# Every batch fetches its expert's weights, in place of looking for the expert in the slots of the last three batches

## The chip, the cores and the metric

The kernel runs on one core of one Trainium2 chip. The metric is the device time of one execution in microseconds (us), the median of several runs. The core's engines are called as in the profile: PE (matmuls) with PEld (its weight loads), DVE, ACT, POOL and SP; POOL, ACT and SP also issue DMAs, all of which run on the core's 16 DMA engines.

## What is computed

Eight batches of 576 tokens go through causal attention with forget gates (8 heads of 64), and each batch's result (576 x 512) through one expert of eight. The expert is chosen once for a whole batch, from the mean of its attention output:

```python
x = attention(q, k, v, f)                  # (8, 576, 512)
pooled = x.mean(axis=1)
logits = pooled @ w_gate                   # (8, 8)
e_idx = argmax(logits, axis=1)             # one expert for a batch
gate_w = softmax(logits)[e_idx]
h = relu(x[b] @ w1[e_idx[b]])              # 512 -> 1024
out[b] = gate_w[b] * (h @ w2[e_idx[b]])    # 1024 -> 512
```

With the inputs of all runs here the eight batches choose the experts 2, 4, 3, 3, 3, 5, 5, 3. An expert has 512 x 1024 weights in w1 and as many in w2, in fp32 in HBM: 4.2 MB, which become 2.1 MB of bf16 in SBUF.

## The kernel before

A batch `b` has two quads `g = 2b, 2b+1` of four heads. The stages of a quad: its K and Q are loaded by POOL's DMA queue (`rawk`, `rawq`, L290, fp32 to bf16 pieces), transposed on DVE (`kt`, `qt`, L406), scores are made on PE in four steps S (`ps_s`, L419), exponentiated on ACT (`e`, L425), masked on POOL (L434; two quads share the masks with DVE, L432), and multiplied by V on PE (P, L459). V (`vf`, loaded from the SP and ACT queues, L302) is first weighed by the forget gates on POOL (`vb`, L443, L446). DVE normalizes into `xT` (L479). After a batch's second quad come the gate (`gate1` to `gate7`: L566, L571, L575, L581, L590), the expert's number in POOL's registers and its weights (`weights1`, L605), then the hidden layer H on PE (L645, with relu on DVE and ACT, L653 and L655), and the output O (L662, L665), which is copied (L672, L674) and stored by SP (L679).

The order on every engine is made when the program is built: `Order.run` (L144) gives each operation a cost, a priority and, for loads, a landing time on shared DMA engines (L107), and takes the best that is ready; the result is a fixed instruction order. Rings of buffers bound how far work runs ahead: four pairs of raw tiles, two of `qt`/`kt`, two of `vf`, three weight slots `w`. Of POOL's order around the weights: `raws[g]` is issued behind the first weighing of V of quad g-2 (L706), and a batch's weights as soon as `gate3` has the expert (L696, priority -5). [...]

Weights live in three slots used in turn. Batch 0 loads w1 in eight pieces (L615) and w2 (L638). Batch 1 has one older batch and simply fetches: `fetch` (L596) issues three DMAs from HBM, two for w1 (L601), one for w2 (L602). From batch 2 on POOL compares the expert with those of up to three batches before, puts the answers together as bits of a number, and switches (L626) over 2, 4 or 8 arms:

```python
        for n in range(1, min(3, b - 1) + 1) if CACHE else ():
            bit = (ev[b] == ev[b - n]) * (1 << (n - 1))
            case = bit if case is None else case + bit
        if case is None:
            fetch(b)
            return
        for arm in tc.Switch({mybir.EngineType.Pool: case}, 1 << min(3, b - 1)):
            if arm == 0:
                fetch(b)
            elif arm < 4:
                z = wslot[b - (1 if arm % 2 else 2)]
                for q in range(2):
                    nc.gpsimd.dma_start(W1[w][:, 2 * q:2 * q + 2, :], W1[z][:, 2 * q:2 * q + 2, :], max_dma_last_dim=2048)
                nc.gpsimd.dma_start(W2[w], W2[z], max_dma_last_dim=2048)
```

Arm 0 fetches; a match one or two batches back copies the slot in SBUF (L632, L633); a match only three batches back needs nothing, since that is the same slot. With the experts above, batch 2 takes arm 0, batches 3, 4 and 6 copy, batch 5 takes arm 0, and batch 7 finds its slot filled. The other engines have a branch for each switch too (L905).

Of the kernel before, what the change touches and what calls it, by code (L numbers as in the profile page):

```python
# [34 lines left out]
MAX_SPAN = 72.0  # L35
COLD = 1.35
HIT = .07
CACHE = 1
VGRAIN = .022

MASKS = (2, 3)
# [190 lines left out]
def fast_path(ctx, tc, q, k, v, f, moe_w_gate, moe_w1, moe_w2, out, flag):  # L232
# [359 lines left out]
    def gate7(op, b):  # L592
        i, ps = od.slot(("gate", b)), PS_W[od.slot(("bank", ("spread", b)))]
        nc.vector.tensor_copy(GATE[i], ps[:, 0:1])
# [10 lines left out]
    def weights1(op, b, a):  # L605
        i, w = od.slot(("gate", b)), od.slot(("w", b))
        if a == 0:
            wslot[b] = w
            assert b < 3 or wslot[b - 3] == w
            ev[b] = nc.gpsimd.value_load(IDX8[i][0:1, 0:1], min_val=0, max_val=NE - 1)  # L610
        if b == 0:
            src = moe_w1[bass.ds(ev[b], 1), :, :].rearrange("o (q p t) n -> p (o q) t n", p=P, t=2)
            parts = W1[w].rearrange("p a (m n) -> p a m n", m=4)
            for q in range(2):
                nc.gpsimd.dma_start(parts[:, a, 2 * q:2 * q + 2, :], src[:, q, :, 256 * a:256 * a + 256])  # L615
            return


        case = None
# [15 lines that stand above are left out]
    def weights2(op, b):  # L635
        w = od.slot(("w", b))
        if b == 0:
            nc.gpsimd.dma_start(W2[w].rearrange("p (a m) n -> p a (m n)", a=4),  # L638
                                moe_w2[bass.ds(ev[b], 1), :, :].rearrange("o (a p m) n -> p (o a) (m n)", a=4, m=2))
# [46 lines left out]
    for b in range(NB):  # L686
# [8 lines left out]
        g7 = od.add(f"g7{b}", "DVE", .1, lambda op, b=b: gate7(op, b), prio=-5, after=[g6], gives=(("bank", ("spread", b)),))  # L695
        ld = lx = od.add(f"W{b}", "POOL", 2.9 if b and CACHE else 1.7, lambda op, b=b: weights1(op, b, 0), prio=-5, after=[g3], takes=(("w", b),), lands=5.4 * (1 - CACHE * HIT * min(3, max(0, b - 1))) if b else 1.5, grain=.17 if b else .05)  # L696
        if b == 0:
            quarters = [ld]
            for a in (1, 2, 3):
                lx = od.add(f"W{b}{a}", "POOL", 1.3, lambda op, b=b, a=a: weights1(op, b, a), prio=-5, behind=[lx], lands=1.5, grain=.05)  # L700
                quarters.append(lx)
        ld2 = od.add(f"w{b}", "POOL", .01 if b else .6, lambda op, b=b: weights2(op, b), prio=-5, behind=[lx], lands=5.3 * (1 - CACHE * HIT * min(3, max(0, b - 1))), grain=.17)
        if b == 0:
# [206 lines left out]
```

## Time and profile before

| what | value |
|---|---|
| median of 3 runs | 280.4 us (278.5 to 281.73) |
| the profiled execution, its own time | 278.5 us |
| its span, first to last instruction | 276.8 us |
| mean granted PE clock | 0.943 |
| busy: PE, ACT, DVE, POOL | 234.4, 167.8, 134.3, 114.9 us |
| HBM read, written | 45.25, 9.44 MB |
| weight fetches from HBM / copies in SBUF / neither | 4 (batches 0, 1, 2, 5) / 3 (3, 4, 6) / 1 (7) |

The span is read as stages by when POOL loads the expert's number (L610): 29.9 us for batch 0, then 53.6, 89.8, 116.8, 145.6, 175.2, 205.1 and 235.5 us for batch 7. After the last one only the FFNs of the last batches remain. In rows of the page "busy" is time in instructions, without waits, branches and DMA issue by the queues; a row's "idle before" names what the engine waited for, and "issue" there means that the profile shows nothing that it waited for.

### The profile page before, as it was taken

The numbers are of one execution on the slowest core, as the hardware profiler recorded it, in microseconds if no ns is written. First come the engines' busy times: TensorE is split into PE (matmuls) and PEld (weight loads), VectorE is DVE, ScalarE is ACT, GpSimd is POOL, SyncE is SP. The second block draws the span as 40 slices with busy tenths as digits, with TensorE's granted clock in tenths as the row PEclk, the third lists the DMA queues.
The fourth block names the chain that finished last, engine by engine and source line by source line (L and its number), as shares of the span: only waits on it lengthen the run. The fifth ranks groups of instructions, "written<-read, shape, count | busy, mean of one in ns | idle before, by whom it ended". The sixth has DMA issues, their size and how long they took to land.

```text
span 276.8 us, 8026 instructions
## 1 busy us (share of the span) xinstructions
PE 234.4 (85%) x3275; PEld 149.4 (54%) x3294; DVE 134.3 (49%) x350; ACT 167.8 (61%) x291; POOL 114.9 (42%) x181
## 2 busy tenths in 40 slices
PE   0889779799989758995999699986999499999991
PEld 0346347545965334771568445773457275794940
DVE  4977875733568613551187315762475153340500
ACT  2677878577638827863758656773577444452530
POOL 4375490051995353136933582439503921000000
PEclk9999999999999965998999979997999779999999
DMA  6994699999999999449893994799726301303132
GB/s 126 225 217 75 103 148 207 228 208 247 264 159 206 192 211 220 75 128 300 170 240 110 289 165 134 161 191 207 177 79 228 118 2 59 116 6 120 51 100 82
DMA packets 56208, 43.92 MB, mean 159 GB/s; under 512 B 39696, under 2 KB 42768, under 8 KB 56144
## 3 DMA queue, kind: packets, MB, share of 16 engines
q0 software_dynamic: 12240, 24.12, 44.3%
q1 hardware_dynamic: 31424, 15.90, 22.2%
q10 hardware_dynamic: 12480, 3.15, 5.7%
q8 instruction: 28, 0.46, 0.7%
q14 instruction: 36, 0.29, 0.4%
HBM read 45.25 MB, written 9.44 MB: 198 GB/s over the span
## 4 chain that ended last, share of the span: by engine, by line
PE 60%; issue 13%; POOL 9%; ACT 7%; DMA 6%; DVE 2%; POOLq 1%; ACTq 0%; DVEq 0%
PE ps_w L662 19%; PE ps_w L645 15%; PE ps_w L459 11%; PE ps_s L419 10%; ACT e L425 6%; POOL e L434 4%; DMA rawk<-in_k_dram 4%; PE ps_w L665 3%; POOL vb L443 2%; DMA w1e<-in_moe_w_dram 2%; POOL w1e L632 1%; DVE xT L479 1%; PE ps_w L571 1%; POOL w2e L633 1%; ACT lr L469 1%
## 5 line engine op out<-in xcount | busy, mean ns | idle before, releaser
L425 ACT ACTIVATE e<-ps_s 128x896 bf16<-128x896 f32 (+2 forms) x128 | 100.0, 833 | 28.0 <-PE ps_s L419 27.4
L645 PE MATMUL ps_w<-xT,w1e 128*128 128x288 bf16 x512 | 73.0, 295 | 1.0 <-DMA w1e<-in_moe_w_dram 1.0
L434 POOL TENSOR_SCALAR_AFFINE_SELECT e<-e 128x512 bf16<-128x512 bf16 (+1 forms) x72 | 42.0, 595 | 63.5 <-ACT e L425 51.9
L645 PEld LDWEIGHTS <-w1e 128*128 128x128 bf16 x512 | 60.5, 140 | 10.8 <-issue 5.4
L662 PE MATMUL ps_w<-w2e,h1T 128*128 128x512 bf16 x238 | 59.4, 385 | 1.8 <-issue 1.3
L419 PE MATMUL ps_s<-qt,kt 32*128 32x448 bf16 (+4 forms) x768 | 47.8, 308 | 12.6 <-DVE mid L368 7.7
L653 DVE TENSOR_SCALAR h1T<-ps_w,gate_b 128x288 bf16<-128x288 f32 x77 | 39.1, 516 | 36.4 <-PE ps_w L645 35.7
L479 DVE SCALAR_TENSOR_TENSOR xT<-ps_w,lr 128x256 bf16<-128x256 f32 (+1 forms) x64 | 27.0, 454 | 48.8 <-PE ps_w L459 26.1
L459 PE MATMUL ps_w<-e,vb 128*32 128x320 bf16 (+4 forms) x1024 | 34.5, 278 | 6.2 <-POOL vb L443 4.2
L662 PEld LDWEIGHTS <-h1T 128*128 128x128 bf16 x256 | 22.7, 98 | 29.2 <-issue 5.7
L419 PEld LDWEIGHTS <-kt 32*128 32x128 bf16 x768 | 20.2, 98 | 33.0 <-issue 21.8
L655 ACT ACTIVATE h1T<-ps_w,gate_b 128x288 bf16<-128x288 f32 x51 | 25.2, 500 | 20.2 <-PE ps_w L645 14.2
L674 ACT COPY otile<-ps_w 128x512 f32<-128x512 f32 (+1 forms) x29 | 16.0, 550 | 30.9 <-PE ps_w L662 27.7
L459 PE MATMUL ps_w<-e,WB 128*32 128x192 bf16 (+4 forms) x512 | 20.4, 269 | 13.3 <-POOL e L434 13.2
L459 PEld LDWEIGHTS <-vb 128*32 128x32 bf16 x1024 | 23.8, 106 | 13.4 <-POOL vb L443 4.7
L443 POOL TENSOR_TENSOR vb<-vf,WF 128x512 bf16<-128x512 f32 x25 | 26.1, 1046 | 2.8 <-ACT WF L380 2.5
L406 DVE STREAM_TRANSPOSE kt<-rawk 128x576 f32<-128x576 f32 (+1 forms) x17 | 21.2, 1248 | 10.1 <-PE ps_s L419 5.3
L464 ACT ACTIVATE lr<-ps_w 128x256 f32<-128x256 f32 (+1 forms) x31 | 12.7, 410 | 20.1 <-PE ps_w L459 19.8
L459 PEld LDWEIGHTS <-WB 128*32 128x32 bf16 x512 | 11.4, 100 | 24.1 <-issue 21.9
L406 DVE STREAM_TRANSPOSE qt<-rawq 128x576 f32<-128x576 f32 (+1 forms) x17 | 21.2, 1248 | 0.1
L672 DVE COPY otile<-ps_w 128x512 f32<-128x512 f32 (+1 forms) x11 | 6.8, 619 | 17.6 <-PE ps_w L662 15.2
L469 ACT ACTIVATE lr<-lr 128x256 f32<-128x256 f32 (+1 forms) x31 | 13.7, 443 | 1.0
(63 smaller groups left out, 117.0 us busy)
## 6 DMA issues: line engine op xcount, KB each, us to landing
out_dram<-otile SPq DMA_DIRECT2D x32, 256.0 KB, 2.3
rawk<-in_k_dram POOLq DMA_DIRECT2D x15, 288.0 KB, 4.7
rawq<-in_q_dram POOLq DMA_DIRECT2D x15, 288.0 KB, 6.6
w2e<-in_moe_w_dram POOLq DMA_DIRECT2D x4, 1024.0 KB, 15.0
vf<-in_v_dram SPq DMA_DIRECT2D x12, 256.0 KB, 9.1
vf<-in_v_dram ACTq DMA_DIRECT2D x12, 256.0 KB, 7.1
w1e<-in_moe_w_dram POOLq DMA_DIRECT2D x6, 512.0 KB, 8.7
w1e<-w1e POOLq DMA_DIRECT2D x6, 512.0 KB, 4.0
```

The lines of the kernel that those rows point to most:

```text
L406: nc.vector.transpose(dst, raw)
L419: nc.tensor.matmul(ps[:, col:col + i1 - i0], kt[32 * h:32 * h + 32, KLO[c]:KLO[c] + P, r], qt[32 * h:32 * h + 32, i0:i1, r], start=(r == 0 ...
L425: nc.scalar.activation(e[:, 2 * n:2 * n + 2, :], PS_S[od.slot(("s", (g, s, n)))][:, :, 0:WIDTH[s]], AF.Exp, scale=0.125)
L434: nc.gpsimd.affine_select(out=x, in_=x, pattern=[[0, 4], [1, n]], channel_multiplier=-1, base=base, compare_op=ALU.is_ge, fill=0.0)
L443: eng.tensor_tensor(vb[:, c, :, :], vf[:, c, h, :], WF[:, b, c, h].unsqueeze(3).to_broadcast([P, 2, 4, D]), op=ALU.mult)
L459: nc.tensor.matmul(ps[32 * h:32 * h + 32, lo - i0:hi - i0], lhs, e[s][:, h, col:col + hi - lo], start=(n == 0), stop=(n == len(parts) - 1) ...
L469: nc.scalar.activation(LR[i][:, 0:w], LR[i][:, 0:w], AF.Exp, scale=-1.0)
L479: nc.vector.scalar_tensor_tensor(XT[od.slot(("x", b))][:, mm, i0:i1], ps[:, 0:i1 - i0], 1.0 if (g, blk) in ON_DVE else LN_SCALE, LR[od.slo ...
L645: nc.tensor.matmul(ps[:, 0:288], lhs, xT[:, m, 288 * half:288 * half + 288], start=(m == 0), stop=(m == 3))
L653: nc.vector.tensor_scalar(dst, ps[:, 0:288], g[:, 0:1], 0.0, op0=ALU.mult, op1=ALU.max)
L655: nc.scalar.activation(dst, ps[:, 0:288], AF.Relu, scale=g[:, 0:1])
L662: nc.tensor.matmul(ps, h[:, j, P * sb:P * sb + P], r, start=(j == 0), stop=(j == 7))
```

## The change

One constant is changed.

```diff
-CACHE = 1
+CACHE = 0
```

It is used in three places. In `weights1` (L620) no comparison is made, `case` stays `None`, and every batch from 1 on calls `fetch`: the switch, its arms and the branches on the other engines are not in the program any more, and neither are the copies. In the planner (L696, L702) the issue of a batch's weights on POOL is costed at 1.7 instead of 2.9, and their landing is no longer shortened for likely matches. The planner therefore makes another order from batch 2 on. The start, up to the fetch of batch 1 and quads 4 and 5, is the same. On POOL, K and Q of quad 9 stood ahead of batch 2's weights and now stand behind them; K and Q of quad 10 stay behind batch 3's weights; at batch 4's weights, Q of quad 12 stood behind and both tiles of quad 12 and K of quad 13 now stand ahead, with Q of 13 behind; at batch 5's weights, both tiles of quad 14 stood behind and now only Q does. On PE the same matmuls are made, in a somewhat different mixing of S, P, H and O; behind the last gate stood 4 O and 16 H of batches 5 and 6 with all of batch 7, and now stand 14 H of batch 6, its O, and all of batch 7.

## Prediction

> **What bounds the kernel now.** First the page: its first line and three rows of its slices (6.9 us each).
>
> ```profile
> span 276.8 us, 8026 instructions
> ...
> PE   0889779799989758995999699986999499999991
> ...
> POOL 4375490051995353136933582439503921000000
> PEclk9999999999999965998999979997999779999999
> DMA  6994699999999999449893994799726301303132
> ```
>
> PE is nearly full from the second slice on, but for dips near slices 13-14, 18, 22, 26-27 and 31. Each is followed by a dip of PE's clock, and POOL is full right after each. DMA is full up to slice 15 and then is not. So PE is the bound, with holes, and the holes have to do with POOL. The waits of PE between 90 and 235.5 us say it outright:
>
> ```profile
> PE ps_w L459 <- POOL e L434: 12.9, 9, 3.6
> PE ps_w L459 <- POOL vb L443: 4.2, 3, 2.7
> ```
>
> 17.1 us in total, and next comes ACT with 1.6 us: P waits for masks and weighed V from POOL. POOL is 42% busy, so it isn't slow but late. Its timeline around batch 1's fetch, which has no switch, and around batch 5's, which is the same three DMAs in arm 0 of a switch:
>
> ```profile
> 54.81 1.44 POOL L601 DMA_DIRECT2D w1e<-in_moe_w_dram  x2 [12.98 <-DVE sumexp L585]
> 56.25 0.76 POOL L602 DMA_DIRECT2D w2e<-in_moe_w_dram  x1
> 57.01 0.65 POOL L434 TENSOR_SCALAR_AFFINE_SELECT e<-e 128x512 bf16<-128x512 bf16 x1
> ```
>
> ```profile
> 177.65 1.49 POOL L601 DMA_DIRECT2D w1e<-in_moe_w_dram  x2 [2.05 <-DVE h1T L653]
> 179.13 0.76 POOL L602 DMA_DIRECT2D w2e<-in_moe_w_dram  x1
> 184.75 0.63 POOL L434 TENSOR_SCALAR_AFFINE_SELECT e<-e 128x512 bf16<-128x512 bf16 x1 [4.87 <-issue]
> ```
>
> Columns: start, length, what. After the same DMAs the next mask follows at once in one case, and after 4.87 us of nothing in the other. A copying arm is slow before its DMAs too. Batch 3, the branch (queue's compare-and-branch rows, first at 118.2), the arm's first instruction (121.7), and the timeline:
>
> ```profile
> L905 POOLq COMPARE_BRANCH  x2: 53/56/58, 118.2 to 123.4; - x2
> ```
>
> ```profile
> L626 POOLq BRANCH_PREFETCH_HINT  x1: 38/38/38, 121.7 to 121.7; - x1
> ```
>
> ```profile
> 122.41 1.49 POOL L632 DMA_DIRECT2D w1e<-w1e  x2 [5.61 <-DVE h1T L653]
> 123.89 0.77 POOL L633 DMA_DIRECT2D w2e<-w2e  x1
> 127.08 1.00 POOL L434 TENSOR_SCALAR_AFFINE_SELECT e<-e 128x512 bf16<-128x512 bf16 x2 [2.42 <-ACT e L425]
> ```
>
> 3.5 us pass between branch and arm, and 2.4 us between its last DMA and the next mask. The "DVE h1T" and "ACT e" in the brackets are only what ended last by the profile; the load of the expert's number had run at 116.8. In the chain of waits these stretches stand as "issue", on the path that sets the end.
>
> **What the Trainium skill says.** "Runtime: NRT & Kernel Launch", section Instruction fetch mechanics: prefetch of instructions is sequential, and a taken branch to a target outside the present window waits for a DMA that fetches it. The trace agrees: 2.5 to 3.5 us into a copying arm, 0.5 us into arm 0, which follows the branch directly, and 2.35 to 4.87 us out of any arm. "TensorE: Matmul & The Clock Gate", Part 1: after an idle window of about 3.4 us the clock is halved, and it takes a busy window to come back. The trace shows half-clock stretches right after the five holes (granted clock 0.55 in 97 to 110.7 us, 0.70 to 0.71 in three of 3.4 us, 0.60 in 216.5 to 223.3). "DMA: Bandwidth & Descriptors", Queues, rings and completion order: each queue is drained in ring order, and the engines alternate between queues; so K and Q that are issued behind a fetch on POOL's queue come after it. The trace agrees: those issued at 37.8 behind batch 0's w2 landed 12.1 us later, against 4.2 us at 129.
>
> **The change part by part.**
>
> *POOL's switches go.* From the load of the expert's number to POOL's next work: batch 1 takes 53.6 to 57.01 = 3.4 us. Batches 2 to 6 take 89.8 to 98.16, 116.8 to 127.08, 145.6 to 155.12, 175.2 to 184.75, 205.1 to 214.22: 8.4, 10.3, 9.5, 9.6, 9.1 us, of which batch 2's load waited 0.7. Less 3.4 each, POOL is free 4.3, 6.9, 6.1, 6.2 and 5.7 us earlier. Batch 7's switch delays nothing, as POOL has no work behind it. PE's holes at these five places, from the stage table (PE busy in 95.0-99.8, 126.4-129.2, 155.1-159.6, 185.7-190.2, 214.1-219.3: 0.81, 0.11, 1.40, 1.21, 1.25), are 4.0, 2.7, 3.1, 3.3, 4.0 = 17.0 us, each smaller than what POOL gains there. So I count them as filled: -17.0 us. The masks still wait 3.4 us for value load and three DMA issues; batch 1 shows that this makes no hole in PE (20.8 busy of 21 us after 54).
>
> *The clock.* In the five half-clock stretches PE is busy 9.9 + 2.1 + 2.4 + 2.5 + 4.4 = 21.2 us; its matmuls there take about 1.5 times as long (462 at most against 286 ns in L645). At full clock 14.1 us, so -7 us if the holes are gone. Bounds: 0 (the clock dips anyway) to -7.
>
> *Branches on PE, ACT, DVE, SP.* Six each of 0.03 to 0.3 us, behind instructions queued on PE: nothing. If not hidden, 1 us on PE.
>
> *Fetches in place of copies.* The DMA view by window prices both, software queue alone: first 178 to 193 us (batch 5's fetch and a little of K and Q), then 209 to 218 us (batch 6's copies). Columns: packets, MB written, share of 16 engines.
>
> ```profile
> q0 software_dynamic: 1215, 2.40, 89.4%
> ```
>
> ```profile
> q0 software_dynamic: 560, 2.10, 62.4%
> ```
>
> A fetch is 15 x 0.894 x 2.10/2.40 = 11.7 us of all 16 engines, the copies 9 x 0.624 = 5.6. Four fetches more (batches 3, 4, 6, 7), three sets of copies fewer: +46.8 - 16.8 = +30 us of DMA work, on 73.3% of 276.8 = 203 now. Batch 7's fetch hides: issued at the last gate it needs about 16 us (177.65 to 193.4 for batch 5's), and PE has 14 H and an O of batch 6 first, some 16 us, before the first half is needed. The other three go into the loaded stretch:
>
> ```profile
> core 0: us, PE busy (x) PEld busy (x) DVE busy (x) ACT busy (x) POOL busy (x), PEclk, DMA share, GB/s
> 35.00:90.00 55.00, 50.31 (x790) 32.52 (x792) 33.21 (x84) 37.86 (x67) 28.88 (x43) 1.00 1.12 209
> 90.00:235.50 145.50, 125.67 (x1893) 79.03 (x1904) 66.22 (x188) 91.27 (x158) 67.83 (x101) 0.89 0.70 165
> 235.50:276.80 41.30, 34.85 (x239) 24.83 (x238) 8.82 (x20) 14.96 (x30) 0.00 (x0) 0.99 0.23 80
> ```
>
> Work from 90 us to the last gate: 145.5 x 0.70 + 3 x (11.7 - 5.6) = 120 us. With 17 + 7 us taken out the stretch has 121.5 us. So DMA would have to run at 0.99 where it showed 1.12 for 55 us in the first row (the times of packets overlap there, hence over 1), with PE still 91% busy. It fits, without room: DMA becomes a second bound.
>
> *K and Q behind fetches.* Quad 9's tiles landed at 92.6 and 95.4; behind batch 2's fetch (last landing 109.9 now) they come at about 113 to 114, plus two transposes of 1.25 us: 116.5. Their first scores stood at 122.2; less the 4 + 4 us that batch 2's hole and clock give back, 114. About 2 us late. Quad 10's: batch 3's fetch would queue behind these and end near 126, tiles 131, transposed 134; scores stood at 143.6, less about 12, plus 3 for H that the new order puts before them: 134.5. Just in time. Quads 13 and 14 have 7 us or so in hand. With contention from V (up to 16.5 us to landing beside a fetch) I take +5 us; bounds 0 and +20.
>
> *New order of PE.* The same matmuls; I take 0, bounds -2 to +3.
>
> Sum against the profiled span: 276.8 - 17.0 - 7 + 5 = 257.8 us. The execution's time was 1.7 us above its span, and the median of the runs 1.9 above that execution: 257.8 + 1.7 + 1.9 = 261.4, say 261 us.
>
> **The rivals.**
>
> *DMA takes back half and more.* If DMA sustains only 0.92 (its share in 90 to 118 us), 120 us of work take 130, the last gate comes at 220 and the end, with 41.3 us behind it, at 262; with late V besides, the gain is 3 to 12 us: 268 to 277. For it: DMA is already at 9 in slices 5 to 15, and nearly the whole stretch would be used. Against it: 1.12 held for 55 us.
>
> *Slower, by quad 9's tiles.* They are the first moved behind a fetch, in the stretch where DMA is full, and everything behind batch 2's fetch is pushed: batch 3's fetch, quad 10, quad 11. If each batch from 2 to 5 then loses 7 us at its scores (tiles landing 9 instead of 2 us late), 28 us outweigh the 24: about 284. It decides when a fetch with its tiles takes over 28 us instead of 20; batch 1's fetch, in the worst crowd, took 20 (54.8 to 74.7).
>
> *No change.* The holes are PE waiting for exponentials that would be late anyhow: 280. For it: POOL waits 34 us for ACT in this stretch. Against: at each hole two to four masks run back to back as soon as POOL returns, so their inputs were there.
>
> **How the numbers follow.** Forecast, 252 to 268: 0.62. DMA takes half, 268 to 277: 0.22. No change, 277 to 283: 0.06. Slower, about 284 and up: 0.10. About 1% is what a measurement of this kernel can tell from no change. So faster 0.84, same 0.06, slower 0.10. The floor is near 250: PE's work behind 90 us at full clock, about 153 us, the 89 before and 6 of last stores. The range of 252 to 276 leaves out the last two cases and a little at its lower end.
>
> **What would show each step.** Right: POOL goes on at once after L602 at every batch; PE waits on POOL under 4 us in the middle stretch; PEclk without dips; DMA share 0.95 and more from 90 us to the last gate; 7 fetches, HBM read 62 MB; a last gate near 213 us. Wrong: idle of DVE's L406 or PE's L419 that a DMA of `rawk` or `rawq` ends, adding to over 10 us; H waiting for `w1e`; or gaps of POOL after L602 that stay, so that they weren't the switch's.

## The result, and the profile after

The kernel after takes 255.3 us (median of 4 runs, 254.19 to 256.45), against 280.12 us before in the same job. The ratio is 0.911, with a 95% interval of 0.905 to 0.918. In a later job on another chip, against other runs of before, it was 0.924 (0.916 to 0.932). The forecast was 261 us with 252 to 276: the way and the mechanism were right, the gain was larger than forecast by 5 to 6 us.

The page of the kernel after, its first line and the same rows of its slices (now 6.3 us each):

```profile
span 252.5 us, 7983 instructions
...
PE   0789799799998995989999999999899999999990
...
POOL 5375285034296298328989332289532581300000
PEclk9999959999999999999999999999999999999998
DMA  6997599999999799995999999979999922499032
```

From slice 16 on (the first is slice 0) PE is at 9 but for two 8s. Of the five valleys of before one is left, the 5 in slice 15. PE's clock has one dip at slice 5, which is in the start that the change doesn't touch and which the page of before doesn't have, and none behind it but at the very end. That is one execution: another one of the same kernel, profiled later (span 256.8 us), has a half-clock stretch behind batch 2's fetch as well, with a mean clock of 0.74 from 90 to 110 us. DMA is now at 9 in most slices up to 31. What PE waits for between 90 us and the last gate (215.9 us):

```profile
PE ps_s L419 <- ACT e L425: 1.9, 3, 1.0
PE ps_w L459 <- POOL e L434: 1.6, 1, 1.6
```

POOL's 17.1 us have become 1.6, in one wait: a mask of quad 6 that ends at 97.9 us. POOL works without a gap from batch 2's fetch at 91.1 up to it: three DMA issues, two masks, two weighings of V, and the issues of quad 9's K and Q. POOL around batch 5's fetch:

```profile
167.47 1.41 POOL L601 DMA_DIRECT2D w1e<-in_moe_w_dram  x2
168.88 0.77 POOL L602 DMA_DIRECT2D w2e<-in_moe_w_dram  x1
169.62 0.56 POOL L290 DMA_DIRECT2D rawq<-in_q_dram  x1
```

Nothing stands in brackets: it goes on at once, as it did only behind batch 1's fetch before. From 90 us to the last gate, and after it (columns as in the stage table of before: us, PE, PEld, DVE, ACT, POOL, granted clock, DMA share, GB/s):

```profile
90.00:216.00 126.00, 119.40 (x1921) 78.26 (x1935) 67.72 (x189) 92.13 (x161) 71.59 (x107) 1.00 0.95 196
216.00:252.50 36.50, 30.39 (x213) 21.97 (x212) 7.69 (x17) 13.67 (x28) 2.21 (x3) 0.97 0.55 132
```

PE is busy 95% of the stretch at full clock, where it was busy 86% at 0.89. The stretch is 19.5 us shorter, and the last one 4.8 us, since the new order has done more of H and O by then. HBM reads are 62.03 MB, as seven fetches need.

The difference of the two spans, 24.3 us, splits by the page's first part: PE's busy time fell from 234.4 to 224.8 us for the same matmuls (9.6 us, which I put down to the clock), and span less PE's busy time fell from 42.4 to 27.7 us (14.7 us, the holes).

### The profile page after: what moved, and what is told of

Same layout as the page of the kernel before. It is cut to its first block, busy times and chain, and to the rows that moved or that the text cites. A ratio compares the mean times of both kernels' runs of the same rounds, so it can differ in the third digit from the quotient of the medians.

```text
span 252.5 us, 7983 instructions
## 1 busy us (share of the span) xinstructions
PE 224.8 (89%) x3272; PEld 145.9 (58%) x3294; DVE 134.5 (53%) x349; ACT 167.3 (66%) x292; POOL 117.3 (46%) x184
## 3 DMA queue, kind: packets, MB, share of 16 engines
HBM read 62.03 MB, written 9.44 MB: 283 GB/s over the span
## 4 chain that ended last, share of the span: by engine, by line
PE 68%; DMA 16%; ACT 6%; DVE 4%; issue 3%; POOLq 0%; ACTq 0%; DVEq 0%; POOL 0%
PE ps_w L645 22%; PE ps_w L662 20%; PE ps_s L419 11%; PE ps_w L459 10%; DMA vf<-in_v_dram 7%; ACT e L425 4%; DMA rawk<-in_k_dram 4%; PE ps_w L665 3%; DMA w1e<-in_moe_w_dram 2%; DMA out_dram<-otile 2%; DVE xT L479 1%; DVE otile L672 1%; PE ps_w L571 1%; PE ps_w L590 1%; DVE qt L406 1%
## 5 line engine op out<-in xcount | busy, mean ns | idle before, releaser
L662 PE MATMUL ps_w<-w2e,h1T 128*128 128x512 bf16 x235 | 57.8, 380 | 2.1 <-issue 1.3
L419 PE MATMUL ps_s<-qt,kt 32*128 32x448 bf16 (+4 forms) x768 | 46.1, 297 | 13.5 <-DVE mid L368 7.5
L653 DVE TENSOR_SCALAR h1T<-ps_w,gate_b 128x288 bf16<-128x288 f32 x71 | 35.8, 514 | 34.0 <-PE ps_w L645 33.4
L479 DVE SCALAR_TENSOR_TENSOR xT<-ps_w,lr 128x256 bf16<-128x256 f32 (+1 forms) x64 | 26.9, 454 | 27.7 <-ACT lr L469 25.1
L655 ACT ACTIVATE h1T<-ps_w,gate_b 128x288 bf16<-128x288 f32 x57 | 28.0, 500 | 19.1 <-PE ps_w L645 16.6
L459 PE MATMUL ps_w<-e,vb 128*32 128x320 bf16 (+4 forms) x1024 | 30.0, 254 | 1.6 <-ACT lr L469 1.1
L674 ACT COPY otile<-ps_w 128x512 f32<-128x512 f32 (+1 forms) x24 | 13.0, 542 | 24.7 <-PE ps_w L662 21.0
L459 PEld LDWEIGHTS <-vb 128*32 128x32 bf16 x1024 | 21.7, 98 | 5.0 <-issue 2.3
L601 POOL DMA_DIRECT2D w1e<-in_moe_w_dram x14 | 10.1, 722 | 26.6 <-DVE kt L406 11.9
L672 DVE COPY otile<-ps_w 128x512 f32<-128x512 f32 (+1 forms) x16 | 10.3, 641 | 22.0 <-PE ps_w L662 17.6
L406 DVE STREAM_TRANSPOSE qt<-rawq 128x576 f32<-128x576 f32 (+1 forms) x17 | 21.2, 1248 | 0.7 <-DMA rawq<-in_q_dram 0.6
L459 PE MATMUL ps_w<-e,WB 128*32 128x192 bf16 (+4 forms) x512 | 18.3, 259 | 2.5 <-POOL e L434 1.8
```

Of the source, the lines that this page charges most:

```text
L406: nc.vector.transpose(dst, raw)
L419: nc.tensor.matmul(ps[:, col:col + i1 - i0], kt[32 * h:32 * h + 32, KLO[c]:KLO[c] + P, r], qt[32 * h:32 * h + 32, i0:i1, r], start=(r == 0 ...
L459: nc.tensor.matmul(ps[32 * h:32 * h + 32, lo - i0:hi - i0], lhs, e[s][:, h, col:col + hi - lo], start=(n == 0), stop=(n == len(parts) - 1) ...
L479: nc.vector.scalar_tensor_tensor(XT[od.slot(("x", b))][:, mm, i0:i1], ps[:, 0:i1 - i0], 1.0 if (g, blk) in ON_DVE else LN_SCALE, LR[od.slo ...
L653: nc.vector.tensor_scalar(dst, ps[:, 0:288], g[:, 0:1], 0.0, op0=ALU.mult, op1=ALU.max)
L655: nc.scalar.activation(dst, ps[:, 0:288], AF.Relu, scale=g[:, 0:1])
```

## The experiments

The theory is that POOL's stalls around the switch made the holes, the holes made most of the clock dips, and the added fetches are hidden. The rivals: the planner's new order brought the gain; the copies themselves cost the time; the fetches do cost something and hide part of the gain.

**The switch with the new order.** The planner's costs are those of the kernel after, the code is that of before.

```diff
 CACHE = 1
+PLAN = 0
```

and `CACHE` becomes `PLAN` where the planner uses it (L696, L702).

> The order of the kernel after on every engine (the planner's costs as after), but with the comparisons, the switch and the copies of before. Theory (POOL's stalls around the switch make the time): the holes of PE behind POOL come back, 274 to 283 us, clock about 0.94. Rival (the new order of PE and POOL brought the gain): 253 to 260 us.

Measured: 277.18 us, ratio to before 1.001 (0.997 to 1.005). PE's waits from 88 to 243 us:

```profile
PE ps_w L460 <- POOL e L435: 16.7, 9, 4.2
...
PE ps_w L460 <- POOL vb L444: 0.5, 1, 0.5
```

(An added line moves the numbers by one: L460 is P, L435 the mask.) The new order with the switch is the kernel before in time and in holes. The order did not bring the gain.

**The old order without the switch.** `PLAN = 1`, and the loop that compares is left out, so every batch fetches.

> The order of the kernel before on every engine (the planner's costs as before), but every batch from 1 on fetches without a switch. Theory (switch): 253 to 260 us, PE waits for POOL under 4 us between 90 us and the last gate, clock about 0.98. Rival (new order): 270 us or more.

Measured: 254.85 us, ratio 0.918 (0.907 to 0.929). PE's waits in the same window:

```profile
PE ps_w L646 <- DMA w1e<-in_moe_w_dram: 2.3, 1, 2.3
...
PE ps_w L460 <- POOL e L435: 0.2, 1, 0.2
```

All of the gain is here. Since these two runs cross code and order, the order is worth nothing that can be measured. One H waits 2.3 us for batch 2's weights, which in the old order stand behind quad 9's K and Q.

**The switch with seven fetches.** Every arm fetches, the order and the comparisons are those of before.

```diff
-            if arm == 0:
+            if arm >= 0:
                 fetch(b)
-            elif arm < 4:
+            elif arm < 0:
```

> The kernel before with its order, comparisons and switch, but every arm fetches from HBM, so there are no copies in SBUF, and seven fetches. Theory (switch): 276 to 288 us, as before or a few us more for the DMA work, holes of PE as before. Rival (it was the copies that cost time, by contention in SBUF or by waiting for the source slot): 255 to 265 us.

Measured: 285.1 us, ratio 1.030 (1.020 to 1.040). PE's waits from 88 to 243 us:

```profile
PE ps_w L459 <- POOL e L434: 15.0, 10, 3.4
PE ps_w L459 <- POOL vb L443: 5.0, 3, 3.4
```

So the copies were not the cost: without them, but with the switch, the time is worse. The holes come to 20.0 us instead of 17.1, and the stalls are longer: behind the last DMA of batches 3, 4, 5 and 6 POOL stands for 4.0, 4.7, 5.5 and 3.9 us, against 2.4, 2.9, 4.9 and 2.4 before. Two things differ there, the DMA load (27 us more of all engines by the pages' shares) and the arms that used to be empty, which now hold a fetch each; this run doesn't separate them.

**Copies without a switch.** The order of the kernel after; which slot is copied is written into the program, and the copies are the three DMAs of before, from slot `wslot[z]`.

```diff
+FROM = {3: 2, 4: 3, 6: 5, 7: None}
...
+        if b in FROM:
+            z = FROM[b]
+            if z is not None:
...
+            return
```

> The kernel after with its order, but batches 3, 4 and 6 copy their slot in SBUF and batch 7 loads nothing, which is written into the program for these inputs; the comparison is left out. It measures what the four more fetches cost the kernel after. Theory (the 30 us of DMA work are hidden): 253 to 257 us, as after. Rival (DMA is a second bound and the fetches cost some 5 us, as I forecast): 248 to 251 us.

Measured: 255.48 us, ratio 0.921 (0.913 to 0.929), the kernel after had 0.911 (0.905 to 0.918) and in the later job 0.924. Taking 31 us of DMA work out again (by the pages' shares, 229.5 to 198.0 us) gains nothing that these intervals of about 1% can tell. This is the run in which my +5 us fail: 5 us would be 2%.

**Two arms.** The comparison is with the batch before alone: `min(1, b - 1)` in place of `min(3, b - 1)`, in the loop and in the number of arms.

> The kernel before, its order, but POOL compares only with the batch before and the switch has two arms in place of two to eight, so the code that a branch has to pass is shorter; for these inputs batches 3, 4 and 6 copy, and batches 2, 5 and 7 fetch. If the stall is that of a branch to a target out of reach, the stalls of batches 3 to 6 shrink and the time goes towards 255 to 268 us. If every taken branch costs 2 to 4 us on POOL wherever it goes, 273 to 280 us.

Measured: 265.97 us, ratio 0.955 (0.947 to 0.963): about half of the gain. PE's waits from 88 to 222 us:

```profile
PE ps_w L459 <- POOL e L434: 9.9, 8, 4.0
```

POOL's timeline at batch 3, which copies, and at batch 5, which fetches:

```profile
121.87 1.48 POOL L632 DMA_DIRECT2D w1e<-w1e  x2 [5.64 <-DVE h1T L653]
123.32 0.77 POOL L633 DMA_DIRECT2D w2e<-w2e  x1
124.08 1.03 POOL L434 TENSOR_SCALAR_AFFINE_SELECT e<-e 128x512 bf16<-128x512 bf16 x2
...
169.38 1.46 POOL L601 DMA_DIRECT2D w1e<-in_moe_w_dram  x2 [1.61 <-DVE row L586]
170.84 0.76 POOL L602 DMA_DIRECT2D w2e<-in_moe_w_dram  x1
175.70 0.63 POOL L434 TENSOR_SCALAR_AFFINE_SELECT e<-e 128x512 bf16<-128x512 bf16 x1 [4.10 <-ACT e L425]
```

The copying arm is now the last one. It is still entered late (the queue's branch at 117.5, the arm's first instruction at 121.2), but the next mask follows its DMAs at once. There is a branch out of this arm too (the queue's second row, at 122.8; POOL has 12 such rows in this kernel as in before). What it costs, if anything, passes under the arm's own DMA issues, which end at 124.08; one packet of instructions is loaded from 121.2 to 122.8 us, under these issues, and none from there to 124.1. The fetching arm is entered at once, and still left by a stall of 4.1 us. So each switch shows one stall in place of up to two, and the stalls that are left are not shorter on the whole (3.7, 2.5 and 2.7 us into the copying arms, against 3.5, 2.5 and 2.5), though the code to pass is. Both of my alternatives were wrong by half: fewer open stalls helped, shorter jumps into and out of the others did not.

**A tiny switch.** The kernel after, plus two arms of one element each ahead of the fetch of batches 2 to 7.

```diff
...
+            if b > 1:
+                for arm in tc.Switch({mybir.EngineType.Pool: ev[b] == ev[b - 1]}, 2):
+                    nc.gpsimd.memset(TINY[:, arm:arm + 1], 0.0)
             fetch(b)
```

> The kernel after with its order and all its fetches, plus, for batches 2 to 7 ahead of the fetch, a comparison with the batch before and a switch of two arms that each only set one element, so that a branch passes four instructions at most. If any taken branch on POOL costs 2.4 to 4.9 us however near its target, each switch adds 3 to 5 us to POOL, PE's holes come back and the time is 258 to 268 us. If a near target costs nothing (the stall is that of far targets, and the two-arm switch was slow for its long arms), 254 to 257 us.

Measured: 282.28 us, ratio to before 1.022 (1.012 to 1.031); the kernel after, in the same job, 256.85 us. So the switch alone, with next to nothing in it and nothing saved by it, costs 25 us: above my 258 to 268. PE's waits from 88 to 245 us, and POOL at batch 2, where the DMA engines are full:

```profile
PE ps_w L460 <- POOL e L435: 20.8, 10, 6.9
```

```profile
90.56 0.09 POOL L627 MEMSET tiny<- 1x1 f32 x1 [0.22 <-issue]
97.61 1.46 POOL L602 DMA_DIRECT2D w1e<-in_moe_w_dram  x2 [6.96 <-issue]
```

Between the two stand the branch out of arm 0, over a handful of instructions, and 6.96 us of nothing. The same branch out of the same arm took 5.36 us at batch 5 and 3.50 us at batch 7; the DMA engines were busy for 0.92, 0.62 and 0.02 of these three stalls. So a near target does not spare the stall: here the measurement goes further than the Trainium skill's "Runtime: NRT & Kernel Launch", section Instruction fetch mechanics, which names the stall for targets outside the window at hand. (Near, if the arms stand in the program one behind the other, as they are written; the trace shows no addresses.) This switch is dearer than the switch of before. A likely reason, which no run separates: the branch out of the arm has no DMA issues to pass under, and the fetch waits for it too (at batch 3 there are 3.3 us into the arm and then 2.8 us up to the fetch).

> The kernel after once more, unchanged, for the comparison on the chip of the run with the tiny switches: 253 to 258 us.

That was the comparison for it: 256.85 us (254.32 to 258.5), ratio 0.924 (0.916 to 0.932).

What comes with these stalls can be counted: instruction packets of 8 KB in the table of DMA queues, before and then after.

```profile
q14 instruction: 36, 0.29, 0.4%
```

```profile
q14 instruction: 15, 0.12, 0.2%
```

All kernels without a switch have 15 (old order, new order, copies or fetches), all with one have 33 to 36, the tiny switch 33. So the switches come with added loads of instructions, by the same DMA engines, 18 to 21 packets over 6 to 10 stalls. They fall into the stalls: each of the nine stalls of the tiny switch has 1 to 4 of them in it. That these loads are what the stall lasts for fits its length growing with DMA load, but it is not shown: a packet took 0.3 to 1.1 us, a stall 2.8 to 7, and no run here takes the load away and keeps the branch.

**Spare matmuls in the holes.** The kernel before, with 65 matmuls on zeros ahead of the P units that waited, so PE isn't idle while it waits.

```diff
...
+        for _ in range(SPARE.get((g, blk, what), 0) if lo_n == 0 else 0):
+            nc.tensor.matmul(ps, still[:, 0:P], still[:, 0:512])
```

> The kernel before with 65 spare matmuls on zeros, put on PE ahead of the P units of quads 6, 8, 10, 12 and 14 where the holes were, of about the length of the holes (14 us in all). The holes stay as waits for POOL, but PE is not idle in them. If the clock dips come from the holes: dips mostly gone, 270 to 275 us (the clock term of about 7 us alone). If the dips have another cause: clock as before, 278 to 284 us.

Measured: 274.01 us, ratio 0.978 (0.970 to 0.986). The granted clock:

```profile
PEclk9999999999999995799999999999999999999997
```

Four of the five dips are gone with the switch still in its place, and 5 to 6 us of time with them (by the medians 4.9, by the ratio 6.2). The dip that stayed follows the longest stretch of waits at batch 2. So those clock dips were the holes' doing, and the clock term of 7 us had about the right size.

**More DMA.** The kernel after, with w1 fetched a second time for each batch into a tile that nobody reads.

```diff
...
+        for q in range(2):
+            nc.gpsimd.dma_start(XTRA.rearrange("p (t q) n -> p q t n", t=2)[:, q], src[:, q])
```

> The kernel after with the expert's w1 fetched twice for batches 1 to 7, the second time into a tile that nobody reads: +5.85 us of all DMA engines for each batch, 41 us in all, and two more DMA issues of 0.72 us each on POOL. Theory (after has little DMA room left, 0.95 and more from 90 us to the last gate): K and Q come late behind the fetches, 262 to 280 us. Rival (DMA is far from a bound): 255 to 259 us.

Measured: 276.32 us, ratio 0.991 (0.989 to 0.994), about 20 us above the kernel after for some 38 us of DMA work (by the pages' shares; 41 were reckoned). The stretch up to its last gate:

```profile
90.00:234.80 144.80, 127.18 (x1950) 81.15 (x1964) 70.03 (x198) 94.94 (x164) 80.72 (x120) 0.94 1.03 208
```

DMA share is 1.03, PE is down to 88% busy, and DVE's transposes now wait for K and Q, from 88 to 236 us:

```profile
DVE qt L407 <- DMA rawq<-in_q_dram: 6.1, 3, 5.7
...
DVE kt L407 <- DMA rawk<-in_k_dram: 5.5, 3, 3.3
```

So the rival that I gave 0.22 is real, and the kernel after stands close to it: 27 us of work fitted, another 38 did not. It has a second face that I had not thought of: around batch 4's fetch POOL's DMA issues are held up by older transfers (1.0 to 2.1 us ahead of each of six), with V and masks behind them. PE waits 4.4 us for masks in this run, against 1.6 us, so not all of the 20 us are late K and Q; each batch also has two DMA issues more on POOL.

**Costs as measured.** The kernel after with 3.3 us for a fetch on POOL and a landing of 12.4 us in the planner (12.1 us by batch 7's fetch in the kernel after, which is nearly alone on the DMA engines).

> The kernel after, with the planner told what the trace shows of a fetch: 3.3 us on POOL in place of 1.7, and a landing of 12.4 us of all DMA engines in place of 10.7. It measures what the order is worth. If PE has no waits left that an order could remove: 253 to 258 us. If the order matters by more than a few us: outside of this on either side.

Measured: 260.68 us, ratio 0.935 (0.928 to 0.942): by the two ratios of the kernel after 1 to 3% worse. Truer costs made no better order; PE waits more for ACT's exponentials in it (6.4 us against 1.9). No run points to a version that beats the kernel after: old order, copies and the kernel after itself lie within each other's spread.

## Why the prediction was right, step by step

- **POOL's switches, -17.0 us: right.** PE's waits for POOL fell from 17.1 to 1.6 us, so 15.5; the crossed runs show that the code and not the order did it. Batch 2's hole was not filled whole: the three DMA issues, of which batch 1 had shown that they make no hole, still cost 1.6 us there. And one reading of the page was wrong: POOL is at 9 or 8 at the end of four of the five valleys, but not after slices 13 and 14 (3 and 1 in slices 15 and 16).
- **The clock, -7 us: right in kind, too small.** PE's busy time fell by 9.6 us, though the profiled execution has a dip of its own in slice 5. The term was sized from the wrong stretches: each was taken 1.4 us too early, so that their granted clock came out at 0.55 to 0.71. In 98.5 to 112.1, 129.2 to 132.6, 159.9 to 163.3, 190.6 to 194.0 and 217.9 to 224.8 us the clock is 0.50 throughout, and PE is busy for 26.8 us in them and not 21.2; with the same factor of 1.5 that makes 8.9 us. Filling the holes gave 5 to 6 us with one dip left, so the forecast's reading (holes make dips) holds. A hole needn't fill the 3.4 us that the prediction names: batch 3's 2.7 us, in the 3.4 us before 129.2, were enough. Batch 2's dip is the uncertain one, as its hole isn't wholly gone: one profile of the kernel after has none there, and one has.
- **Branches on the other engines, nothing: not contradicted.** No wait on PE shows them; they were not tried alone.
- **Fetches in place of copies, hidden: right.** The price about held: all queues together rose by 27 us of all engines, from 73.3% of 276.8 us to 90.9% of 252.5 us, where 30 were forecast. The share in the stretch is 0.95 (0.99 by the sum, 0.95 and more among the signs), the last gate came at 215.9 us (forecast 213). Batch 7's w1 had landed at 225.0 when its H began at 230.7, its w2 at 232.0 when its O began at 238.6.
- **K and Q behind fetches, +5 us: the term that was mis-sized; it is 0.** Quad 9's tiles landed at 111.0 and 112.8 (forecast 113 to 114), and DVE had transposed them by 115.6. But their scores stood at 117.6 and not at 114. I had taken 4 us of batch 2's hole and 4 us of clock off the old time; up to these scores, behind as many matmuls (391 from 90 us on), PE's busy time fell by 3.5 us, but its idle time only from 5.6 to 4.5, as batch 2's hole was not filled whole. DVE waited once for `rawk`, 1.5 us, for quad 8's K ahead of the fetch, and PE not at all. Quad 10's tiles came at 135.3 (forecast 131), its scores at 139.3 (forecast 134.5): both late by the same 4 to 5 us. And the +5 was a sum over sites none of which I had shown to be late by more than 2 us. The run with copies puts the cost of the added fetches at nothing that can be measured.
- **The sum.** -15.5 of waits, -9.6 of clock, 0 in place of +5, and +0.8 of other idle time of PE make the 24.3 us of the spans; forecast were 19.
- **The rival on the slower side** needed quad 9's tiles 9 us late; they came before they were wanted. The rival "no change" fell with the old order without the switch.

## What to carry to other kernels

Price a branch at run time by the stall of the engine that takes it and by what is queued behind it, not by the instructions or bytes that it saves: here a switch that saved 27 us of hidden DMA work held up the masks and cost 25 us. Where a saving is in a resource with room, ask what the saving's own control code does on an engine that feeds the bound. And before adding an allowance for contention, check place by place that something would be late; a +5 that no place shows is a guess.

## What was not expected of the hardware

- A taken branch on POOL, as I read the rows, stalled it for 2.4 to 7 us where nothing covered it, out of arms of one small instruction as out of long ones. In the tiny switch the least was 2.8 us, with the DMA engines busy 0.01 of the time, and the most 6.96 us, with 0.92.
- A branch that is not taken costs little: 0.4 us from batch 5's branch to its arm (176.4 to 176.8), against 3.5 us for batch 3's (118.2 to 121.7).
- PE matmuls on zeros, put where PE would wait, gained 2.2% (1.4 to 3.0), with the granted clock at 0.974 in place of 0.943, though they do no work.
- POOL's DMA issues can be held up by older transfers of the same queue: 0.6 us once in the kernel after, with 27 us more DMA work than before, 1.0 to 2.1 us at each of six issues in a row with 64 us more.
